# Masks and query decays of a retention layer: loaded tables, or products of small factors made on chip

## The chip, the cores and the metric

The kernel runs on one core of one Trainium2 chip. The metric is the device time of one execution in microseconds (us), the median of several runs. A core has five engines with their own instruction streams: TensorE (PE in the rows, its weight loads PEld), VectorE (DVE), ScalarE (ACT), GpSimd (POOL) and SyncE (SP), which here issues most of the DMAs. They meet at semaphores. TensorE writes its products into PSUM, eight banks of 512 numbers per partition; VectorE and ScalarE read them there.

## The reference, cut to what matters

The first layer is a retention (a linear attention with decay) over 4 batches, 8 heads, 576 positions and 64 features; two feed-forward layers follow (512 to 2048 and back, 2304 tokens).

```
scores = scale * q @ k.T                       # per batch and head
gamma  = 1.0 - 2.0 ** (-5.0 - arange(H))       # one decay per head
Dmat   = where(rel >= 0, gamma ** rel, 0.0)    # rel = row - column
x = (scores * Dmat) @ v                        # then heads side by side: 2304 x 512
h = x @ w_in;  g = max(0.01 * h, h);  x = g @ w_out
h = max(x @ w_in2, 0.0);              out = (h * h) @ w_out2
```

## The kernel before, in words

**Retention.** Each batch is cut into chunks, four of 128 positions and one of 64, so there are 20 chunks, and the loop goes over them in order (variable `i`). Within a chunk the scores of all heads are products of keys and queries (`scores`, L513), multiplied on VectorE by a mask that holds `gamma ** (t - s)` for s <= t and zero elsewhere (L515). Earlier chunks of the batch come in through a state per head, the sum of `k v` products (`sums`, L550, copied by ScalarE to `state`, L556). For that the keys are multiplied by `gk` (L528) and the queries by `gq` (L524), both on GpSimd. `gq` has one table for each chunk number 1 to 4 in a batch: `gamma ** (c * 128 + t)` times the scale. `output` adds the masked scores times values (L541) and the queries times state (L544) in one bank, and ScalarE copies it to `ysb` (L559), the input of the feed-forward layers.

**Tables.** Mask, `gq` and `gk` are computed on the host and loaded: the mask at L473, each `gq` at L470, `gk` at L477. The mask is 128 x 1024 numbers, a `gq` 128 x 512 (the last 128 x 256).

**Feed-forward.** The weights arrive as 64-bit floats and are taken apart by VectorE and ScalarE into high and low parts (`steps_in` L149 to L187, `steps_out` L191 to L216), in small steps that are spread among the chunks: `RATE` says how many steps stand behind a chunk, and `FIRST = 3` steps stand in front of the first. The first block of weights lands in `ysb`'s last third, which is still free (L128), and the later ones in `raw`. The feed-forward products (L318, L419) take three products per pair of operands; their operands are built by `operands` (L256 to L281), partly during the retention.

**Order.** The instructions of each engine run in the order of the program text; nothing reorders them. Each DMA in turn takes one of eight semaphores, and waits for the one that had it before. SP issues all DMAs here except the first three key loads, which ScalarE issues. Before the first scores TensorE makes products of a zero tile (`keep_warm`, L466), and again before the outputs of chunks 0 and 1; `WARM` holds the numbers.

**Banks.** Scores use two pairs of banks in turn (`wide`), sums have one bank for themselves. Output and warm-up products take the other three in turn, y1 to y3, and a tile that takes a bank waits until the reader of the last tile there is done:

```
def bank(name="yps", i=None):
    if i is None:
        i = turn[0] = turn[0] % 3 + 1 if att else (turn[0] + 1) % 4
    return psum.tile([P, 512], F32, tag=f"y{i}", name=name)
```

In the order of the calls warm-up products get y1, y2, output 0 y3, warm-up y1, output 1 y2, output 2 y3, output 3 y1. A product of 32-bit floats is carried out as two passes, so eight score products are 16 instructions in the trace.

Of the kernel before, what the change touches and what calls it, by code (L numbers as in the profile page):

```python
# [13 lines left out]
AF = mybir.ActivationFunctionType  # L14
# [3 lines left out]
B, H, S, D = 4, 8, 576, 64  # L18
NT, DM, DFF = B * S, H * D, 2048
P = 128  # L20
# [8 lines left out]
FULL = S // P  # L29
C = NP * P  # L30
# [5 lines left out]
DEEP = 4  # L36
# [4 lines left out]
ARRIVE = 3  # L41
FIRST = 3
AHEAD = 2
WARM = 10, 3, 1
BIGGEST = float(np.uint32(0x0FEFFFFF).view(np.float32))

A22, A11, A12, S1, S2, S3, S4 = range(7)


@with_exitstack  # L50
def retention_ffn_kernel(ctx: ExitStack, tc: tile.TileContext, full, rows, half, halfv, w1, w2, const, mask, gk, out):

# [9 lines left out]
    nc = tc.nc  # L64
    sub, mul, add, mx = ALU.subtract, ALU.mult, ALU.add, ALU.max
# [7 lines left out]
    ysb = [keep.tile([P, NK * 2 * HT], F32, name=f"ysb{i}") for i in range(NB)]  # L73
# [5 lines left out]
    def wide(i, name=None):  # L79

        return psum.tile([P, 2, 512], F32, tag="ab"[i], name=name or "ab"[i])
# [227 lines left out]
    def product(ps, ws, w, use, start):  # L309

        x = xs.pop(use)
        used[0] += 1
        for u in range(NU):
            hi, lo = ws[u]
            for k in range(2):
                s = slice(k * P, (k + 1) * P)
                for i, (a, b) in enumerate(((hi, 0), (hi, 1), (lo, 0))):
                    nc.tensor.matmul(  # L318
                        ps[:, u, :HT], a[:, w, s], x[:, b, k],
                        start=(start and k == 0 and i == 0), stop=(k == 1 and i == 2), skip_group_check=True,  # L320
                    )
        load_x()
# [122 lines left out]
    def tokens(i):  # L445
        b, c = chunks[i]
        return b * S + c * P, P if c < FULL else S - FULL * P

    class Retention:
# [15 lines left out]
                for _ in range(n):  # L465
                    nc.tensor.matmul(ps[:, :P], self.cold, self.cold, start=True, stop=True)  # L466

        def load_gq(self, c):
            src = const[c - 1].rearrange("p (a t) -> p a t", t=P)
            nc.sync.dma_start(self.gq[c - 1], src[:, :, : self.gq[c - 1].shape[2]])  # L470

        def load_mask(self):
            nc.sync.dma_start(self.mask.rearrange("p j a t -> p (j a t)"), mask)  # L473
            nc.vector.memset(self.state, 0.0)

        def load_gk(self):
            nc.sync.dma_start(self.gk.rearrange("p c h -> p (c h)"), gk)  # L477
# [90 lines left out]
    def run(n, limit):  # L568

        while n > 0 and done[0] < limit:  # L570
            if next(steps, None):
                break
            done[0] += 1
            n -= 1

    def build(n=1):

        ran = 0
        while builds and ran < n:
            try:  # L580
                if next(builds[0]):
                    break
                ran += 1
            except StopIteration:
                builds.pop(0)
        return ran

    GROUP = NU * (STEPS_IN + STEPS_OUT)
    with tc.manual_schedule():
        with tc.tile_pool(name="att", bufs=1) as pool:  # L590
            att.append(Retention(pool))
            ret = att[0]
            n = len(chunks)
            ret.load(0)
            ret.load_mask()
            ret.load_rows(0)
            ret.load_gk()
            weights.ahead()
            ret.load(1)
            ret.load_rows(1)  # L600
            ret.load_gq(1)
            ret.load(2)
            ret.load_rows(2)
            ret.load_gq(2)
            ret.load(3)
            ret.load_rows(3)
            ret.load_gq(3)
            ret.keep_warm(WARM[0])
            ret.scores(0)
            ret.decay(0)  # L610
            run(FIRST, GROUP)
            scored = 1
            for i in range(n):
                if i + DEEP < n:
                    ret.load(i + DEEP)
                    ret.load_rows(i + DEEP)
                    if i + DEEP <= FULL:
                        ret.load_gq(i + DEEP)
                if weights.loads < GRP and (weights.free or i == 1):
                    weights.free = False  # L620
                    weights.ahead()

                while scored < n and scored <= i + (AHEAD if i > 2 else min(i, 1)):
                    ret.scores(scored)
                    ret.decay(scored)
                    scored += 1
                ret.keep_warm(WARM[i + 1] if i + 1 < len(WARM) else 0)
                ret.output(i)
                a, t = tokens(i)
                if a < 2 * HT <= a + t:  # L630
                    builds.append(operands(0, 0))
                run(min(1, RATE[i]), GROUP - OWN)
                if BUILD[i] > 0:
                    build()
                run(RATE[i] - 1, GROUP - OWN)
                build(BUILD[i] - 1)
                if i >= n - 3 and i < n - 1:

                    early.append(wide(i - n + 3))
                    product(early[-1], [wt_in[0, 0], wt_in[0, 2]], (A11, A12)[i - n + 3], uses[i - n + 3], True)  # L640
                    if i == n - 3:
                        sums1 = stage.tile([P, NU, HT], F32, tag="t2", name="s")
                        nc.scalar.activation(sums1, early[0][:, :, :HT], AF.Copy)
                    else:
                        early.append(sums1)
# [12 lines left out]
        for layer in range(2):  # L658
            for g in range(NG):
                i = layer * NG + g  # L660


                start = i * GROUP + GROUP
# [46 lines left out]
def constants():  # L710

    gamma = (1.0 - 2.0 ** (-5.0 - np.arange(H, dtype=np.float32))).astype(np.float64)
    scale = 1 / np.sqrt(D)
    row, col = np.arange(P)[:, None], np.arange(C)[None, :]
    gq = [gamma[row // D + 2 * (col // P)] ** (c * P + col % P) * scale for c in range(1, FULL + 1)]
    since = col % P - row
    mask = [np.where(since >= 0, gamma[2 * (col // P) + j] ** np.maximum(since, 0) * scale, 0) for j in range(2)]
    gk = gamma ** -(np.arange(FULL)[:, None] * P + row[:, :, None]).astype(np.float64)
    return [a.astype(np.float32) for a in (np.stack(gq), np.concatenate(mask, axis=1), gk.reshape(P, -1))]


# [42 lines left out]
```

## Time and profile before

| | |
|---|---|
| median of 3 runs | 840.95 us (840.44 to 841.79) |
| the profiled execution: time, span | 840.44 us, 840.4 us |
| TensorE busy | 824.5 us (98%) |
| VectorE busy | 601.4 us (72%) |
| ScalarE busy | 340.2 us (40%) |
| GpSimd busy | 44.3 us (5%), all in the first 80 us |
| DMA over the span | 191.01 MB, 227 GB/s on average |

The time of an execution is its span, so nothing lies around it. The retention takes about the first 85 us; in it GpSimd works, and the DMA engines carry the inputs. The busy shares are averages over both stages, and TensorE's share is above 9 tenths in all but the first of 40 slices.

### The profile page before, as it was taken

Reading aid. Unit: us, or ns where it says so; the run is one execution under the profiler, and the core shown is the slowest. Engines: PE = TensorE matmul, PEld = TensorE weight load, DVE = VectorE, ACT = ScalarE, POOL = GpSimd, SP = SyncE. Lnnn points to the kernel's source line nnn. Section 1 sums busy time; section 2 is a strip of 40 time slices with the busy share of each in tenths; the row PEclk is TensorE's granted clock in tenths of the full one; section 3 lists DMA queues with packets and bytes.
Section 4 is the critical chain, followed back from the end, with each engine's and each line's share of the span. In section 5 each row is a group of like instructions: output and inputs, shape, how many; then the busy total and the mean of one; then the engine's idle time right before and its main releaser. Section 6 shows DMA issues by size and latency. Waiting matters only on the chain.

```text
span 840.4 us, 12382 instructions
## 1 busy us (share of the span) xinstructions
PE 824.5 (98%) x5084; PEld 776.9 (92%) x5084; DVE 601.4 (72%) x734; ACT 340.2 (40%) x447; POOL 44.3 (5%) x36
## 2 busy tenths in 40 slices
PE   7999999999999999999999999999999999999998
PEld 6888899999999999999999998998998998998996
DVE  4698789657666566658668879868777778754534
ACT  1454667544523433434425365543322333321211
POOL 3755000000000000000000000000000000000000
PEclk8999999999999999999999999999999999999999
DMA  9898463967646637746823554966855655735811
GB/s 349 330 322 292 170 258 114 420 250 260 247 180 250 248 135 292 259 140 233 307 101 122 191 226 163 385 246 233 296 178 203 263 182 231 263 140 199 288 51 75
DMA packets 45688, 191.01 MB, mean 227 GB/s; under 512 B 5696, under 2 KB 6720, under 8 KB 45632
## 3 DMA queue, kind: packets, MB, share of 16 engines
q1 hardware_dynamic: 45200, 189.44, 60.7%
q8 instruction: 40, 0.66, 0.3%
q10 hardware_dynamic: 432, 0.79, 0.3%
q14 instruction: 16, 0.13, 0.0%
HBM read 152.45 MB, written 37.75 MB: 226 GB/s over the span
## 4 chain that ended last, share of the span: by engine, by line
PE 84%; DVE 9%; ACT 3%; DMA 2%; issue 2%; SPq 0%; DVEq 0%; ACTq 0%
PE yps L419 44%; PE a L318 21%; PE b L318 15%; DMA raw<-in_w 1%; DVE r L515 1%; PE ops L544 1%; ACT sf L149 1%; PE ops L541 1%; DMA ysb<-in_w 1%; DVE x L260 1%; PE scps L513 1%; DVE sf L163 1%; DVE ilo L187 1%; PE sums L550 1%; DVE sf L205 1%
## 5 line engine op out<-in xcount | busy, mean ns | idle before, releaser
L318 PE MATMUL a<-x,ihi 128*128 128x384 f32 x768 | 196.1, 336 | 2.7 <-DVE t L384 2.4
L318 PE MATMUL b<-x,ihi 128*128 128x384 f32 x576 | 146.6, 335 | 0.8 <-DVE t L370 0.8
L318 PEld LDWEIGHTS a<-x,ihi 128*128 128x128 f32 x768 | 138.5, 188 | 5.8 <-DVE t L384 4.0
L419 PE MATMUL yps<-ghi,ohi 128*128 128x384 f32 x384 | 128.6, 335 | 0.6 <-ACT ysb L428 0.6
L318 PE MATMUL a<-x,ilo 128*128 128x384 f32 x384 | 128.5, 335 | 0.0
L419 PE MATMUL yps<-ghi,olo 128*128 128x384 f32 x384 | 128.3, 334 | 0.0
L419 PE MATMUL yps<-glo,ohi 128*128 128x384 f32 x384 | 128.3, 334 | 0.0
L356 DVE TENSOR_TENSOR glo<-t,ghi 128x768 fp32r<-128x768 f32 x96 | 91.7, 955 | 46.1 <-ACT ghi L351 45.6
L430 DVE TENSOR_TENSOR ysb<-yps,ysb 128x384 f32<-128x384 f32 (+1 forms) x126 | 76.0, 610 | 62.5 <-PE yps L419 62.1
L419 PE MATMUL yps<-ohi,glo 128*128 128x512 f32 x288 | 112.3, 390 | 0.0
L419 PE MATMUL yps<-olo,ghi 128*128 128x512 f32 x288 | 112.3, 390 | 0.0
L419 PE MATMUL yps<-ohi,ghi 128*128 128x512 f32 x288 | 112.1, 389 | 0.0
L351 ACT ACTIVATE ghi<-t 128x768 fp32r<-128x768 f32 x96 | 81.1, 845 | 68.5 <-DVE t L329 55.1
L318 PEld LDWEIGHTS b<-x,ihi 128*128 128x128 f32 x576 | 103.8, 188 | 1.7 <-DVE t L370 1.1
L344 ACT ACTIVATE s<-a 128x768 f32<-128x768 f32 x47 | 38.2, 814 | 156.2 <-PE a L318 156.1
L318 PE MATMUL b<-x,ilo 128*128 128x384 f32 x288 | 96.3, 334 | 0.0
L419 PEld LDWEIGHTS yps<-ghi,ohi 128*128 128x128 f32 x384 | 72.1, 188 | 1.6 <-ACT ysb L428 0.9
L318 PEld LDWEIGHTS a<-x,ilo 128*128 128x128 f32 x384 | 72.1, 188 | 0.0
L419 PEld LDWEIGHTS yps<-glo,ohi 128*128 128x128 f32 x384 | 72.1, 188 | 0.0
L419 PEld LDWEIGHTS yps<-ghi,olo 128*128 128x128 f32 x384 | 72.1, 188 | 0.0
L419 PEld LDWEIGHTS yps<-ohi,glo 128*128 128x128 f32 x288 | 54.0, 188 | 11.3
L419 PEld LDWEIGHTS yps<-olo,ghi 128*128 128x128 f32 x288 | 54.1, 188 | 11.0
(67 smaller groups left out, 997.3 us busy)
## 6 DMA issues: line engine op xcount, KB each, us to landing
x<-x SPq DMA_DIRECT2D x168, 768.0 KB, 5.9
raw<-in_w SPq DMA_DIRECT2D x62, 512.0 KB, 5.0
kv<-in_rows SPq DMA_DIRECT2D x16, 512.0 KB, 5.8
out<-ysb SPq DMA_DIRECT2D x18, 256.0 KB, 2.0
q<-in_full SPq DMA_DIRECT2D x16, 256.0 KB, 4.5
kt<-in_full SPq DMA_DIRECT2D x13, 256.0 KB, 4.7
ysb<-in_w SPq DMA_DIRECT2D x2, 512.0 KB, 6.8
kt<-in_full ACTq DMA_DIRECT2D x3, 256.0 KB, 5.6
```

What stands on the lines that cost most here:

```text
L149: nc.scalar.activation(f32(a), f32(raw[:, :, 1]), AF.Abs)
L163: nc.vector.scalar_tensor_tensor(a, high, 1 << 31, a, ALU.bitwise_and, ALU.bitwise_or)
L187: nc.vector.tensor_tensor(lo[:, a:z], sf[:, a + 1 : z + 1], f32(hi[:, a:z]), sub)
L205: nc.vector.scalar_tensor_tensor(rest, high, 23, low, ALU.logical_shift_left, ALU.bitwise_or)
L260: nc.vector.tensor_tensor(t[:, 1], src, f32(t[:, 0]), sub)
L318: nc.tensor.matmul(ps[:, u, :HT], a[:, w, s], x[:, b, k], start=(start and k == 0 and i == 0), stop=(k == 1 and i == 2), skip_group_check= ...
L344: nc.scalar.activation(t, ps[:, :, :HT], AF.Copy)
L351: nc.scalar.activation(h, t, AF.Copy)
L356: nc.vector.tensor_tensor(l, t, f32(gs[key][0]), sub)
L419: nc.tensor.matmul(acc, a, b, start=(j == u == i == 0), stop=(j == 1 and u == NU - 1 and i == 2))
L430: nc.vector.tensor_tensor(y, acc, y, add)
L513: nc.tensor.matmul(ps[:n, j, p, :n], k[s, c], q[s, c], start=True, stop=True)
```

## The change

The mask and the four `gq` tables are no longer loaded. Two small arrays are: `rank`, 8 partitions (one per head) by 1280 numbers, and `tri`, a 128 x 128 triangle of ones and zeros. Both lie in the second third of `ysb` until its rows are needed. Since `gamma ** (t - s)` is `gamma ** -s` times `gamma ** t`, a product over the 8 partitions, with zeros for the other heads, gives the whole table: `make_mask` makes two such products of 512 columns in a pair of banks, and VectorE multiplies them by the triangle into the mask. `make_gq(c)` makes one product of 512 columns in bank y3, and ScalarE copies it into `gq`. The mask and the first `gq` are made before chunk 0; `gq` 2, 3 and 4 are made after the outputs of chunks 0, 1 and 2. The first group of warm-up products has six instead of ten. Lines behind L474 move by 13 and later ones by more: scores are L526, outputs L554 and L557, sums L563, and ScalarE's copies L569 and L572.

```
-WARM = 10, 3, 1
+WARM = 6, 3, 1
...
-        def load_gq(self, c):
-            src = const[c - 1].rearrange("p (a t) -> p a t", t=P)
-            nc.sync.dma_start(self.gq[c - 1], src[:, :, : self.gq[c - 1].shape[2]])
-
-        def load_mask(self):
-            nc.sync.dma_start(self.mask.rearrange("p j a t -> p (j a t)"), mask)
+        def load_factors(self):
+            n = rank.shape[1]
+            self.rank, self.tri = ysb[1][:H, :n], ysb[1][:, n : n + P]
+            nc.sync.dma_start(self.rank, rank)
+            nc.scalar.dma_start(self.tri, tri)
             nc.vector.memset(self.state, 0.0)
+
+        def make_mask(self):
+            ps = wide(1, "mask")
+            for j in range(2):
+                nc.tensor.matmul(ps[:, j], self.rank[:, j * P : (j + 1) * P], self.rank[:, -C:], start=True, stop=True)
+            ps = ps.rearrange("p j (a t) -> p (j a) t", t=P)
+            tri = self.tri.unsqueeze(1).to_broadcast([P, H, P])
+            nc.vector.tensor_tensor(self.mask.rearrange("p j a t -> p (j a) t"), ps, tri, mul)
+
+        def make_gq(self, c):
+            ps = bank("decay", 3)
+            nc.tensor.matmul(ps, self.rank[:, (1 + c) * P : (2 + c) * P], self.rank[:, -C:], start=True, stop=True)
+            t = self.gq[c - 1]
+            nc.scalar.activation(t, ps.rearrange("p (a t) -> p a t", t=P)[:, :, : t.shape[2]], AF.Copy)
...
+            ret.load_factors()
             ret.load(0)
-            ret.load_mask()
             ret.load_rows(0)
...
             ret.load_rows(1)
-            ret.load_gq(1)
             ret.load(2)
             ret.load_rows(2)
-            ret.load_gq(2)
             ret.load(3)
             ret.load_rows(3)
-            ret.load_gq(3)
             ret.keep_warm(WARM[0])
+            ret.make_mask()
             ret.scores(0)
+            ret.make_gq(1)
             ret.decay(0)
...
-                    if i + DEEP <= FULL:
-                        ret.load_gq(i + DEEP)
...
                 ret.output(i)
+                if 2 + i <= FULL:
+                    ret.make_gq(2 + i)
...
+    rank = [(head % 2 == j) * gamma[:, None] ** -t for j in range(2)]
+    rank += [(head % 2 == t // D) * gamma[:, None] ** (c * P) for c in range(1, FULL + 1)]
+    rank += [(head // 2 == col // P) * gamma[:, None] ** (col % P) * scale]
+    tri = np.arange(P)[:, None] <= t
```

TensorE's first instructions, before (a name is that of the tile written, behind the arrow those read; scps are scores, cold the warm-up products, x10 is ten in a row):

```order
L466 MATMUL cold<-cold 128x128 x10
L513 MATMUL scps<-q,kt 128x128 x8
L466 MATMUL cold<-cold 128x128 x3
L541 MATMUL ops<-r,kv 64x128 x8
L550 MATMUL sums<-kv 64x64 x8
L513 MATMUL scps<-q,kt 128x128 x16
L466 MATMUL cold<-cold 128x128
L541 MATMUL ops<-r,kv 64x128 x8
```

And of the change, where decay is the product for a `gq` table:

```order
L466 MATMUL cold<-cold 128x128 x6
L478 MATMUL mask<-ysb_67 128x512 x2
L526 MATMUL scps<-q,kt 128x128 x8
L485 MATMUL decay<-ysb_67 128x512
L466 MATMUL cold<-cold 128x128 x3
L554 MATMUL ops<-r,kv 64x128 x8
L563 MATMUL sums<-kv 64x64 x8
L485 MATMUL decay<-ysb_67 128x512
L526 MATMUL scps<-q,kt 128x128 x16
L466 MATMUL cold<-cold 128x128
L554 MATMUL ops<-r,kv 64x128 x8
```

Two mask products stand in front of the first scores, a decay product behind them, and another between the sums of chunk 0 and the scores of chunks 1 and 2.

TensorE from the output of chunk 2 to the scores of chunks 4 and 5, before, with the semaphores that an instruction waits on (the number behind a name is that of one buffer):

```order
L541 MATMUL ops_260<-r_209,kv_109 64x128 [waits DMAHW5_49,DVE_49,Activation_49]
L541 MATMUL ops_260<-r_209,kv_109 64x128 x7
L544 MATMUL ops_260<-q_105,state_83 128x128 [waits Activation_49,Pool_49]
L544 MATMUL ops_260<-q_105,state_83 128x128 x3
L550 MATMUL sums_84<-kv_109 64x64 [waits Pool_49]
L550 MATMUL sums_84<-kv_109 64x64 x7
L513 MATMUL scps_293<-q_146,kt_147 64x64 [waits DMAHW4_49,DMAHW3_49,PE_49]
```

And of the change:

```order
L554 MATMUL ops_266<-r_212,kv_109 64x128 [waits DMAHW5_49,DVE_49,Activation_49]
L554 MATMUL ops_266<-r_212,kv_109 64x128 x7
L557 MATMUL ops_266<-q_105,state_83 128x128 [waits Pool_49]
L557 MATMUL ops_266<-q_105,state_83 128x128 x3
L563 MATMUL sums_84<-kv_109 64x64 [waits Pool_49]
L563 MATMUL sums_84<-kv_109 64x64 x7
L485 MATMUL decay_290<-ysb1_67 128x512 [waits PE_49,Activation_49]
L526 MATMUL scps_302<-q_147,kt_148 64x64 [waits DMAHW2_49,DMAHW1_49]
```

The fourth decay product stands in front of the scores of chunk 4 and waits for ScalarE (Activation), which reads bank y3.

ScalarE of the change, from the first `gq` copy on:

```order
L487 ACTIVATE gq_77<-decay 128x512
L149 ACTIVATE sf<-ysb_68 128x1024
L569 ACTIVATE state<-sums 64x4x64 x2
L572 ACTIVATE ysb_66<-ops 128x4x128
L487 ACTIVATE gq_78<-decay 128x512
L569 ACTIVATE state<-sums 64x4x64 x2
L572 ACTIVATE ysb_66<-ops 128x4x128
L487 ACTIVATE gq_79<-decay 128x512
L569 ACTIVATE state<-sums 64x4x64 x2
L572 ACTIVATE ysb_66<-ops 128x4x128
L487 ACTIVATE gq_80<-decay 128x256
```

Each of the later `gq` copies stands behind the state and output copies of a chunk; the first one stands in front of the conversion of the first weight block (L149).

## Rows read from the trace of the kernel before

**Rows 1.** Head of the page.
```profile
span 840.4 us, 12382 instructions
```

**Rows 2.** Busy time by stretch: stretch and length, each engine's busy time, clock, DMA.
```profile
38.90:71.30 32.40, 31.72 (x504) 28.12 (x504) 32.25 (x30) 14.62 (x29) 20.77 (x16) 1.00 0.83 287
85.00:840.00 755.00, 747.38 (x4036) 708.67 (x4034) 538.20 (x674) 303.95 (x379) 0.00 (x0) 1.00 0.58 216
```

**Rows 3.** Chain of waits, first 40 us: start, length, engine or DMA.
```profile
2.60 7.17 DMA ysb<-in_w
...
11.13 1.14 ACT sf L149
...
13.74 2.30 DVE sf L163
16.05 1.15 DVE r L515
...
17.24 1.98 PE ops L541 x16
...
22.27 1.58 PE scps L513 x16
23.85 1.02 PE ops L541 x16
...
26.57 1.70 PE scps L513 x32
28.28 1.02 PE ops L541 x16
...
31.01 1.09 PE scps L513 x16
```

**Rows 4.** Busy time by stretch, 10 to 23.2 us, engines PE, PEld, DVE, ACT, POOL.
```profile
10.00:12.80 2.80, 1.73 (x32) 1.43 (x32) 0.51 (x1) 2.77 (x4) 0.00 (x0) 1.00 1.03 408
12.80:16.40 3.60, 1.61 (x20) 1.30 (x18) 3.53 (x4) 0.72 (x2) 2.70 (x2) 1.00 1.04 410
16.40:23.20 6.80, 5.96 (x48) 5.29 (x50) 4.55 (x4) 0.77 (x3) 2.78 (x3) 0.50 1.08 377
```

**Rows 5.** DMA issues, first 20 us: count, KB each, us to landing.
```profile
gq<-in_const SPq DMA_DIRECT2D x3, 256.0 KB, 6.7
mask<-in_mask SPq DMA_DIRECT2D x1, 512.0 KB, 5.2
...
gq<-in_const SPq DMA_DIRECT2D x1, 128.0 KB, 6.0
```

**Rows 6.** Timeline of TensorE, first 7.3 us: start, length, instruction.
```profile
1.05 4.63 PE L466 MATMUL cold<-cold 128*128 128x128 f32 x20 [1.05 <-DVE cold L459]
5.62 1.42 PE L513 MATMUL scps<-q,kt 64*128 64x128 f32 x16
```

**Rows 7.** Groups by line and form, TensorE, 1 to 5.5 and 6.9 to 8 us.
```profile
L466 PE MATMUL cold<-cold 128*128 128x128 f32 x20 | 4.6, 429 | 1.1 <-DVE cold L459 1.1
...
L466 PE MATMUL cold<-cold 128*128 128x128 f32 x6 | 0.9, 292 | 0.0
```

**Rows 8.** DMA issues of the page: count, KB each, us to landing.
```profile
out<-ysb SPq DMA_DIRECT2D x18, 256.0 KB, 2.0
```

**Rows 9.** Line L487, first 30 us: query and key loads to landing.
```profile
DMA to landing us min/median/max: 3.6/5.8/6.9
```

**Rows 10.** Timeline of VectorE and ScalarE, 7 to 28 us.
```profile
7.08 1.23 DVE L515 TENSOR_TENSOR r<-scps,mask 128x1024 f32<-128x1024 f32 x1 [5.54 <-PE scps L513]
...
26.68 0.78 ACT L556 ACTIVATE state<-sums 64x256 f32<-64x256 f32 x2 [2.90 <-PE sums L550]
27.49 0.60 ACT L559 ACTIVATE ysb<-ops 128x512 f32<-128x512 f32 x1
```

**Rows 11.** Waits, first 40 us: total, times, longest.
```profile
PE scps L513 <- DMA q<-in_full: 2.6, 2, 1.5
...
PE ops L541 <- DVE r L515: 1.3, 1, 1.3
```

More of the change, by code (lines that the diff above doesn't have):

```diff
@@ L50, in retention_ffn_kernel @@
 @with_exitstack
-def retention_ffn_kernel(ctx: ExitStack, tc: tile.TileContext, full, rows, half, halfv, w1, w2, const, mask, gk, out):
+def retention_ffn_kernel(ctx: ExitStack, tc: tile.TileContext, full, rows, half, halfv, w1, w2, rank, tri, gk, out):
     nc = tc.nc
@@ L714, in constants @@
     row, col = np.arange(P)[:, None], np.arange(C)[None, :]
-    gq = [gamma[row // D + 2 * (col // P)] ** (c * P + col % P) * scale for c in range(1, FULL + 1)]
-    since = col % P - row
-    mask = [np.where(since >= 0, gamma[2 * (col // P) + j] ** np.maximum(since, 0) * scale, 0) for j in range(2)]
+    head, t = np.arange(H)[:, None], np.arange(P)[None, :]
+    rank = [(head % 2 == j) * gamma[:, None] ** -t for j in range(2)]
+    rank += [(head % 2 == t // D) * gamma[:, None] ** (c * P) for c in range(1, FULL + 1)]
+    rank += [(head // 2 == col // P) * gamma[:, None] ** (col % P) * scale]
+    tri = np.arange(P)[:, None] <= t
     gk = gamma ** -(np.arange(FULL)[:, None] * P + row[:, :, None]).astype(np.float64)
-    return [a.astype(np.float32) for a in (np.stack(gq), np.concatenate(mask, axis=1), gk.reshape(P, -1))]
+    return [a.astype(np.float32) for a in (np.concatenate(rank, axis=1), tri, gk.reshape(P, -1))]
 def kernel(q, k, v, moe_w_in, moe_w_out, moe2_w_in, moe2_w_out):
@@ L745, in weights @@
         return np.stack([a, w_out.reshape(NF, P, DM)], axis=1).view(np.int64)
-    const, mask, gk = constants()
+    rank, tri, gk = constants()
     arrays = {
@@ L750 @@
         "w1": weights(moe_w_in, moe_w_out), "w2": weights(moe2_w_in, moe2_w_out),
-        "const": const, "mask": mask, "gk": gk,
+        "rank": rank, "tri": tri, "gk": gk,
     }
```

## The prediction

> **What bounds the kernel now.** I read the page first: the span is 840.4 us [rows 1]. Then the busy time by stretch: from 85 us to 840 us TensorE is busy 747.4 of 755 us at the full clock [rows 2], and the change has no instruction there. So whatever it wins or loses it wins or loses before 85 us, as an earlier or later start of that stage, and the reader should expect microseconds, not per cents. Within the front part, VectorE is full from 38.9 to 71.3 us (32.25 of 32.40 us busy) [rows 2]; the change adds no VectorE work there, so this stretch is shifted as a block by whatever happens before it. That leaves the first 38 us.
>
> There I read the chain of waits [rows 3]. It runs over the landing of the first weight block (9.77 us), ScalarE's conversion (11.13), VectorE's three steps (to 16.05), the score multiply of chunk 1 that stands behind them on VectorE, and from 17.24 us over TensorE alone: output, state and sums of chunk 1 to 22.27, scores of chunk 3 to 23.85, output of chunk 2 to 26.57, scores of chunks 4 and 5 to 28.28, output of chunk 3. None of the replaced tables ends a wait on this chain; they sit in front of other transfers. The third thing is the clock: it is full in 10 to 16.4 us, though TensorE is busy there only 1.73 of 2.8 us and then 1.61 of 3.6 us, and it is 0.50, the 1.2 GHz level, from 16.4 to 23.2 us [rows 4]. The same output, state and sums that take 5.03 us for chunk 1 (17.24 to 22.27) take 2.72 us for chunk 2 (23.85 to 26.57) [rows 3]. The low clock costs the chain 2.3 us there and about 0.5 us in the scores behind (1.58 against 1.09), together 2.8 us.
>
> **The change part by part.** All times below are for the profiled execution, whose time is its span, 840.44 us; the median of the runs is 840.95 us, 0.5 us above, and I add that at the end.
>
> Transfers. Removed: the mask, 512 KB, and the decay tables, three of 256 KB and one of 128 KB [rows 5]; 1408 KB in all. Added: rank, 8 rows of 1280 numbers (40 KB), and tri (64 KB). The DMA engines are full and move about 410 GB/s [rows 4], so the first weight block, behind the mask in the queue, lands (512 - 104) KB / 410 GB/s = 1.0 us earlier. ScalarE's conversion goes from 11.13 to about 10.1 us and VectorE's steps end near 15.0 instead of 16.05 (part of it less if GpSimd, now later, leaves VectorE alone). Later loads come up to 3 us earlier, but after 17.24 us no DMA ends a wait on the chain, so that is worth nothing.
>
> Warm-up and mask products. Ten warm-up products take 4.63 us from 1.05 us [rows 6], 0.46 us each, two passes each, 429 ns a pass against 292 ns for the three products of 6.96 us [rows 7]: the page shows no level before 6 us, but the passes show the low one. The 16 score passes at 5.62 us take 1.42 us [rows 6] against about 1.16 in the record of later chunks (1.09 on the chain [rows 3]), so the clock rises near 6.1 us. Six products end near 3.7 us. A factor product has 512 columns, four times a warm-up product: 4 x 0.46 = 1.85 us at the low level, 0.93 at the full one. Two of them for the mask: from 3.75 to 6.1 us at the low level (64% of 3.70), the rest at the full one, end at 6.8. They need rank in time. Its landing has no row; the bounds are the 2.0 us from issue to landing of an output store with the queues nearly empty [rows 8] and the 3.6 us of the first 256 KB load [rows 9], so between 2.7 and 4.3 us for an issue at 0.74. I take 3 us, nearer the small one: before 3.7, no wait. The upper end costs 0.6 us.
> The Trainium skill (DMA: Bandwidth & Descriptors, Anatomy of one DMA, a fit for transfers that GpSimd issues) has about 2.0 us fixed plus the bytes over 436 GB/s: an estimate of 2.1 us for 40 KB, which would land rank at 2.8 us. No row here shows so small a load on an empty queue; by that rule the sum stays as it is, and the upper end of 0.6 us falls away.
>
> VectorE then multiplies the mask out of the product banks by the triangle: same shape and kind as the score multiply of 1.23 us [rows 10]; 6.95 to 8.2. Chunk 0's scores (1.09) are done at 7.9; its score multiply follows at 8.2 to 9.4, where before it began at 7.08 [rows 10]. The cover for that delay is the wait for the weight block.
>
> Decay products. The first (0.93) stands behind the scores: 8.8. ScalarE copies it (0.60, as the copy of an output [rows 10]), three warm-up products end at 9.6, output of chunk 0 runs 9.65 to 10.7, sums to 11.3. Now the banks matter. The copies of the decay product all use product bank 3, and output takes banks 1 to 3 in turn; chunk 0 and chunk 2 get bank 3. So the second decay product waits until ScalarE has copied the state (0.78) and the output (0.60) of chunk 0 [rows 10]: 11.3 + 0.1 + 0.78 + 0.60 + 0.15 = 12.95, end 13.9. Behind it on TensorE wait scores 1 and 2: 14.95 and 16.0. GpSimd's decay of query and key of chunk 1 follows scores 1, about 1 us later than now, with some tenths to spare. VectorE's score multiply 1 goes from 15.1 to 16.3; output 1 starts at **16.35 instead of 17.24: 0.9 us won**.
>
> The clock. TensorE now has the mask, decay products and earlier scores between 6 and 16 us: from 9.65 to 16.35 it idles only 1.7 and 0.1 us, against waits of 2.6 us (two, for queries) and 1.3 us (for the score multiply) in the same stretch before [rows 11]. I take it that the clock stays full: output, state and sums of chunk 1 take 2.72, to 19.07. **2.3 us won, and 0.5 in the scores.**
>
> The given back. Output 2 (bank 3) waits for the copy of decay product 3, which ScalarE makes after state (0.78) and output (0.60) of chunk 1: 0.1 + 0.78 + 0.60 + 0.60 + 0.15 + gaps = 2.3 us after the sums, 21.4; TensorE alone would need 0.93 + 1.09 = 2.0. It replaces the 1.58 between 22.27 and 23.85. Output 2 to sums 2: 2.72, 24.1. The fourth decay product waits for output 2's copy out of bank 3: 0.1 + 0.78 + 0.60 + 0.15 = 1.65, then 0.93: 26.7. Here nothing covers it, since TensorE had no wait here. Scores 4 and 5: 1.70, output 3 at **28.4 against 28.28**.
>
> So 0.9 + 2.3 + 0.5 = 3.7 us are won, and 3.8 are lost: 1.2 on the way to output 2 (2.3 for the 1.09 of the scores at the full clock) and 2.6 before the scores of chunk 4 (1.65 + 0.93). The sum is +0.1 us. From there everything is a shift of the same work. Forecast 840.44 + 0.1 = 840.5 for an execution like the profiled one, **841.0 at the median**. Bounds: with a column rate of the factor products 8% better (a product without its tail) and VectorE's long step at less than 2.30 us [rows 3], 0.6 us less; with rank late and GpSimd late, 0.9 more. Its own range is 840.3 to 842.0.
>
> **Rivals.**
> A. The clock falls as before, between 16 and 23 us. For it: the new idle places, 1.7 us before decay product 2 and 1.65 before product 4, are each longer than any single one of before (1.5 [rows 11]). Against: the work around them is denser than in the stretch that kept its clock at 1.73 of 2.8 us [rows 4]. Then chunk 1's part takes 5.03: 16.35 to 21.4; decay 3 at the low level 1.85, scores about 1.3: output 2 at 24.6, +2.72, +1.65 + 0.93 + 1.70 = 31.6 against 28.28: 3.3 us slower, 844.2. It decides from the point where the clock at output 1 is 0.50. This is the slower side.
> B. The clock rises late. If it is not up by 10 us, mask products end at 7.45, scores 0 at 9.1, decay 1 and the warm-up products at about 11.2, and with the bank wait output 1 starts near 17.9 instead of 16.35: 1.6 us, 842.5, more if it stays low longer. For it: six products instead of ten, and factor products that fill 8 of 128 rows. Against: TensorE has no longer pause than before in its first 6 us.
> The Trainium skill (TensorE: Matmul & The Clock Gate, What's actually happening) says that the low rate is the default and activity releases it; the 429 ns passes agree. Whether products with 8 rows count as such, no row here shows; if not, B holds.
> C. The bank waits are not on the path (ScalarE done early, or TensorE ahead elsewhere). Then output 3 starts at 16.35 + 2.72 + 0.93 + 1.09 + 2.72 + 0.93 + 1.70 = 26.4, 1.8 us earlier: 839.1, just faster by more than 0.2%. For it: ScalarE is little used here. Against: state and output copies can only start when the sums are done.
> D. The tables were hidden and so are their replacements: 840.95.
>
> **How the numbers follow.** 0.2% is 1.7 us, about what a measurement of this kernel can tell from no change. Forecast 0.49, A 0.17, B 0.12, C 0.17, D 0.05. Faster: C with most of its chance, and a tail of the forecast in which rank, mask and VectorE's steps all come early: 0.21. Slower: A, half of B, and a tail: 0.26. Same: 0.53. The time is the forecast's, 840.9 with D beside it. For 8 in 10 the range reaches to C below, 838.8, and to A above, 844.0.
>
> **What would show it.** Right: the clock at 1.00 from 6 to 30 us, mask products over near 6.8, output 1 near 16.4, a wait of TensorE of about 1.6 us in front of decay products 2 and 4 with ScalarE's output copy as releaser, output 3 near 28.3, and VectorE full after 39 as before. Wrong: 0.50 between 16 and 23 (A), low passes after 7 us (B), no wait before decay product 4 (C), or a chain that leaves the first 30 us for something that starts later, such as a load that lands out of its new order.

## The result: one per cent slower, and the profile after

| | before | after |
|---|---|---|
| median, 4 runs each | 841.04 us (840.44 to 841.79) | 849.24 us (848.39 to 851.24) |
| span of the profiled execution | 840.4 us | 846.6 us |

The ratio is 1.0100, with a 95% interval of 1.0088 to 1.0112: slower by 8.2 us at the median, and 5.2 us above the top of the predicted range. The profiled executions are 6.2 us apart. The other 2 us are a choice of executions: in all runs listed here the time is 1.8 us above the span (848.39 us against 846.6 us here), so by this estimate the profiled execution of before [rows 1] took about 842.2 us, 1.2 above its median, and that of after lies 0.85 below its own. The sentence ahead of the prediction that nothing lies around the span is wrong by these 1.8 us.

Head of the page of the changed kernel:

```profile
span 846.6 us, 12392 instructions
```

Busy time by stretch of the changed kernel, columns as in [rows 2] (stretch and length; PE, PEld, DVE, ACT, POOL busy with instructions; granted clock; DMA share and GB/s):

```profile
4.20:7.50 3.30, 3.30 (x21) 1.73 (x21) 1.37 (x2) 0.00 (x0) 0.00 (x0) 1.00 1.05 408
7.60:21.20 13.60, 12.10 (x80) 8.83 (x80) 5.77 (x6) 3.68 (x6) 3.60 (x4) 0.50 1.04 403
21.20:31.40 10.20, 8.64 (x104) 6.21 (x102) 7.47 (x7) 3.20 (x8) 5.65 (x4) 1.00 0.66 211
31.50:34.80 3.30, 3.30 (x38) 2.96 (x36) 1.12 (x2) 0.27 (x1) 1.72 (x2) 0.50 0.28 110
...
45.00:78.00 33.00, 32.15 (x508) 28.49 (x508) 32.64 (x30) 15.49 (x31) 21.43 (x15) 1.00 0.84 288
...
91.00:846.00 755.00, 747.33 (x4036) 708.68 (x4034) 538.01 (x674) 303.85 (x379) 0.00 (x0) 1.00 0.59 216
```

The last two lines answer to [rows 2]: VectorE is still full in its stretch, and the long stage takes the same 747.3 of 755 us. The whole difference is a later start, as expected. The first four lines answer to [rows 4], and there it is: 0.50, the 1.2 GHz level, for 13.7 us from 7.55 to 21.20 us, and again from 31.4 to 34.9 us, where before had one such stretch of 6.8 us. TensorE was not idle ahead of the first fall: it was busy in all 3.30 us from 4.2 to 7.5 us, and went on without a pause to 12.9 us.

Chain of waits of the changed kernel, first 36 us, answering to [rows 3] (start, length, engine, tile and line):

```profile
3.98 2.00 PE mask L478 x4
5.99 1.09 PE scps L526 x16
7.08 1.50 PE decay L485 x2
8.58 1.58 PE cold L466 x6
10.15 1.91 PE ops L554 x16
12.06 0.88 PE sums L563 x16
...
13.77 0.61 ACT ysb L572
...
14.42 2.07 PE decay L485 x2
16.48 3.71 PE scps L526 x32
20.20 0.72 PE cold L466 x2
20.92 1.18 PE ops L554 x16
...
23.80 1.05 PE decay L485 x2
24.85 1.09 PE scps L526 x16
25.95 1.02 PE ops L554 x16
...
30.23 1.12 PE decay L485 x2
31.35 2.96 PE scps L526 x32
34.31 1.30 PE ops L554 x16
```

The weight block and VectorE's three steps, which open this chain before, are gone from it. TensorE carries it from 1.05 us, with two visits to ScalarE (13 to 14.4 us, and the same in front of 30.23 us). Output 3 starts at 34.31 us instead of 28.28 [rows 3]: 6.0 of the 6.2 us between the spans. The decay product for chunk 2 takes 2.07 us, the next one 1.05; the 32 score passes at 16.48 take 3.71.

Timeline of VectorE and ScalarE in the changed kernel, answering to [rows 10] (start, length, engine, line, operation; in brackets idle time and what ended it):

```profile
6.03 1.23 DVE L481 TENSOR_TENSOR mask<-mask,ysb 128x1024 f32<-128x1024 f32 x1 [4.49 <-PE mask L478]
7.36 1.23 DVE L528 TENSOR_TENSOR r<-scps,mask 128x1024 f32<-128x1024 f32 x1
13.18 1.23 DVE L163 SCALAR_TENSOR_TENSOR sf<-ysb,sf 128x1024 uint32<-128x1024 uint32 x1
18.54 1.22 DVE L528 TENSOR_TENSOR r<-scps,mask 128x1024 f32<-128x1024 f32 x1 [4.13 <-PE scps L526]
...
2.60 1.28 ACT L487 ACT_TABLE_LOAD   x1 [2.60 <-issue]
10.56 1.14 ACT L149 ACTIVATE sf<-ysb 128x1024 f32<-128x1024 f32 x1 [1.35 <-DMA ysb<-in_w]
```

And the row of ScalarE's timeline in the kernel before that answers to the last two:

```profile
9.84 1.28 ACT L149 ACT_TABLE_LOAD   x1 [9.84 <-DMA ysb<-in_w]
```

The mask is there in time (output 0 does not wait for it), VectorE is done with the weight block at 14.4 us and then waits 4.13 us for TensorE's scores: the wait for the block became a wait for TensorE.

Waits of the changed kernel, first 60 us, answering to [rows 11] (engine and line, what it waited for, total us, times, longest):

```profile
PE decay L485 <- ACT ysb L572: 3.1, 2, 1.6
```

The two bank waits are real, and of the predicted length.

### The profile page after: what moved, and what is told of

Same layout as the page of the kernel before. It is cut to its first block, busy times and chain, and to the rows that moved or that the text cites. A ratio compares the mean times of both kernels' runs of the same rounds, so it can differ in the third digit from the quotient of the medians.

```text
span 846.6 us, 12392 instructions
## 1 busy us (share of the span) xinstructions
PE 832.6 (98%) x5088; PEld 779.8 (92%) x5088; DVE 601.3 (71%) x735; ACT 342.3 (40%) x451; POOL 45.9 (5%) x36
## 4 chain that ended last, share of the span: by engine, by line
PE 86%; DVE 8%; ACT 3%; issue 2%; DMA 1%; SPq 0%; DVEq 0%; ACTq 0%
PE yps L419 44%; PE a L318 21%; PE b L318 15%; PE scps L526 1%; DMA raw<-in_w 1%; PE ops L554 1%; PE ops L557 1%; DVE r L528 1%; ACT sf L149 1%; DVE x L260 1%; PE decay L485 1%; DVE ilo L187 1%; PE cold L466 1%; PE sums L563 1%; DVE sf L205 1%
```

## The experiments

After the result two reasons stood against each other. Theory 1, the clock: the mask and decay products fill 8 of 128 rows, and the claim is that TensorE's clock neither rises nor stays up behind such products. Its rival, the banks: the two waits for bank 3 make the chain longer, and the clock falls because TensorE pauses there. Differences below are medians against the median of before measured beside them (841.34, 840.58 and 840.51 us, 18 to 25 runs each); the change stands at +8.2 against its own four runs of before. Each record of the clock is that of one profiled execution.

**Rank over all 128 rows (e1).** The same products with zeros in the other 120 rows; `rank`'s load grows by this, and two memsets come with it.

```
-            self.rank, self.tri = ysb[1][:H, :n], ysb[1][:, n : n + P]
-            nc.sync.dma_start(self.rank, rank)
+            self.rank, self.tri = ysb[1][:, :n], ysb[1][:, n : n + P]
+            nc.sync.dma_start(self.rank[:32], rank)   # rows 8 to 31 are zeros
+            nc.vector.memset(self.rank[32:64], 0.0)
+            nc.gpsimd.memset(self.rank[64:], 0.0)
```

> The changed kernel with the factor products made over 128 rows instead of 8 (rank padded with zeros, the table values are the same); columns, number and order of products, bank waits and warm-up stay. Theory 1 (products that fill 8 rows do not hold the clock up): the clock that rose near 4 us stays at 1.00 through 7 to 30 us, decay product 1 takes about 0.9 instead of 1.5 us, output of chunk 3 starts near 28.4 instead of 34.3 us, and the time falls by 5 to 6 us, to within 1.5 us of the kernel before. Rival 2 (the idle waits for bank 3, or six instead of ten warm-up products, bring the clock down): the low stretch 7.5 to 21 us stays, the time stays within 1 us of the changed kernel, 7 to 8 us above the kernel before.

Measured: 844.13 us (842.78 to 848.13), ratio 1.0033 [1.0015, 1.0052]; +2.8 instead of +8.2. Busy time by stretch of this kernel:

```profile
4.00:14.20 10.20, 6.52 (x61) 4.12 (x61) 3.74 (x4) 2.95 (x5) 1.04 (x1) 1.00 1.01 373
14.25:17.60 3.35, 3.35 (x14) 1.85 (x16) 1.27 (x2) 0.60 (x1) 0.00 (x0) 0.50 1.05 402
```

And its timeline of TensorE:

```profile
6.93 1.13 PE L487 MATMUL decay<-ysb 128*128 128x512 f32 x2
...
14.18 2.06 PE L487 MATMUL decay<-ysb 128*128 128x512 f32 x2 [3.12 <-ACT ysb L574]
...
28.58 1.12 PE L487 MATMUL decay<-ysb 128*128 128x512 f32 x2 [1.56 <-ACT ysb L574]
29.64 1.77 PE L528 MATMUL scps<-q,kt 64*64 64x64 f32 x32
```

The clock now stays up past 7.55 us, and falls at 14.22 us, behind a pause of 3.12 us, for one short stretch. In front of the fourth decay product there is the same pause of 1.56 us as in the change, but the scores behind it take 1.77 us instead of 2.96: no fall. So the clock part of theory 1 held in this profile, and the size of what is won back was missed: 2.8 us remain. Four of the ten executions have a mean clock of 1.000 and still took 843.1 to 843.5 us, so about 2 us of the rest are no fall of the clock. Part of them the padding made itself: the weight block was issued at 3.96 us instead of 3.13, behind the landing of `tri` (`rank` beside it has 160 KB now instead of 40), ScalarE's conversion came at 11.72 us, and it stands in front of the copies that free bank 3.

**Other banks for the decay products (e2).** Rows as in the change; no pause before products 2 and 4.

```
-            ps = bank("decay", 3)
+            ps = bank("decay", (3, 2, 1, 2)[c - 1])
```

> The changed kernel with the decay products in banks 3, 2, 1, 2 instead of always 3, so that none waits for an output copy; rows stay 8. Theory 1: the clock still falls near 7.5 us and stays low to about 20 us, since nothing changes before; the waits of 1.5 us before decay products 2 and 4 go, 2 to 3 us of the 6 to 8 are won back, time 4 to 6 us above the kernel before. Rival 2 (the idle waits bring the clock down): at least the second low stretch at 31 us goes and the first is shorter than half, time within 2 us of the kernel before. A loss that was only the waits themselves: 3 us won back, clock rows unchanged.

Measured: 843.51 us (842.44 to 846.28), ratio 1.0024 [1.0009, 1.0039]; +2.2. Timeline of TensorE:

```profile
3.91 3.78 PE L478 MATMUL mask<-ysb 8*128 8x512 f32 x4
...
15.70 1.12 PE L485 MATMUL decay<-ysb 8*128 8x512 f32 x2
...
27.93 1.77 PE L526 MATMUL scps<-q,kt 64*64 64x64 f32 x32
29.63 1.09 PE L554 MATMUL ops<-r,kv 128*64 128x128 f32 x16
```

Nothing waits for a bank. The clock is low from the start (the four mask passes take 3.78 us, in the change 2.08) until 15.3 us and then stays up, behind the fourth decay product too. Theory 1 was missed here: it had 4 to 6 us left over, and 2.2 is close to what its rival named (within 2 us, no second fall). By the median other banks bring back as much as 128 rows. They do it in another way: both reach output 1 at the same time (19.34 us in e1, 19.28 in e2), but e1's chain comes over the late weight block and ScalarE's copies, and e2's over TensorE alone from 1.05 us, at the low clock until 15.3; from there e2 has no bank wait and is at output 3 by 29.63 us, e1 at 31.34. Of the second fall the profiles say: 8 rows without the pause did not bring it (e2), the pause without the 8 rows did not (e1), both together did (the change). For e2 all eight executions bear this out, with mean clocks of 0.999 and 1.000. Two of e1's ten have 0.995, lower than its profile's 0.998, and where the clock fell in them is not recorded.

**Both (e3).** The two edits above in one kernel.

> Both edits: factor products over 128 rows, and decay products in free banks. Theory 1: clock 1.00 from about 5 us on, no wait of TensorE for ScalarE's output copy, output of chunk 3 near 26.5 us against 28.3 before, time 1 to 2 us below the kernel before (839 to 840). Rival 2: no better than the banks edit alone.

Measured: 844.45 us (841.88 to 846.41), ratio 1.0033 [1.0013, 1.0053]; +3.1. The expectation was missed: the two repairs do not add up. Timeline of TensorE:

```profile
3.78 3.33 PE L480 MATMUL mask<-ysb 128*128 128x512 f32 x4
...
22.42 1.77 PE L487 MATMUL decay<-ysb 128*128 128x512 f32 x2
...
27.94 1.13 PE L487 MATMUL decay<-ysb 128*128 128x512 f32 x2
...
30.70 1.09 PE L556 MATMUL ops<-r,kv 128*64 128x128 f32 x16
```

The clock of this profile is that of before almost to the half microsecond (0.50 from 16.92 to 23.75 us, before 16.42 to 23.25), and output 3 starts at 30.70 us, in the same view of before at 28.21. What is left over are the decay products on TensorE's own path: the third takes 1.77 us, most of it at the low level, the fourth 1.13; 2.9 us together, more than the 2.5 that output 3 is late. Four of the five executions have a mean clock of 0.996 or 0.997; the fifth, with 0.999, took 841.88 us.

**Warm-up products over 8 rows in the kernel before (e4).** No table is touched.

```
-                nc.tensor.matmul(ps[:, :P], self.cold, self.cold, start=True, stop=True)
+                nc.tensor.matmul(ps[:, :P], self.cold[:H], self.cold[:H], start=True, stop=True)
```

> The kernel before (tables loaded) with its fourteen warm-up products over 8 rows of the zero tile instead of 128; nothing else changes, the output is the same. Theory 1: the passes stay at the low level (429 ns) through the ten products and the first scores, and the clock is still low when output of chunk 0 runs at 8.5 us, where before it was full from about 6 us; time 0 to 4 us above the kernel before. Rival 2 (columns and gaps count, not rows): the clock rises near 6 us as before and the time is the same.

One run: 840.52 us (-0.8). Timeline of TensorE:

```profile
5.61 2.08 PE L513 MATMUL scps<-q,kt 64*128 64x128 f32 x16
...
9.19 1.98 PE L541 MATMUL ops<-r,kv 128*64 128x128 f32 x16
...
14.33 1.16 PE L513 MATMUL scps<-q,kt 64*128 64x128 f32 x16 [0.30 <-DMA q<-in_full]
...
24.48 1.09 PE L541 MATMUL ops<-r,kv 128*64 128x128 f32 x16
```

The same twenty passes, back to back from 1.05 to 5.6 us, and six more at 7.62 us, over 8 rows instead of 128: the clock comes up at 14.05 instead of 6.18 us. With the twenty passes over 128 rows it also came up at 6.36 us in e6 and at 5.09 in e10 (both below); over 8 rows there is this one execution. The operands are zeros in both kernels, so here the difference lies in the rows a product takes in, not in the numbers. And the second half: the time, as far as one execution tells, is no worse. The clock stays up from 14.05 us on, and output 3 starts at 24.48, 3.7 us earlier than in the profile of before; the span is 1.7 us shorter, since TensorE then waits for a key load until 28.79 us. The low clock of the first 14 us is not on the path here: the chain of this execution runs over loads up to that point. The fall from 16.4 to 23.3 us was on the path of before.

**Mask half alone (e5), decay half alone (e6).** e5 makes the mask from factors with six warm-up products, and loads the `gq` tables; e6 loads the mask, has ten warm-up products, and makes the `gq` tables as the change does.

```
e5:  -            ret.make_gq(1)
     +            ret.load_gq(1)         # 2 to 4 likewise, where before has them
e6:  -            ret.make_mask()        # and the mask's load back; first load(0), then the factors
     -WARM = 6, 3, 1
     +WARM = 10, 3, 1
```

> Half of the change: the mask made from factors (8 rows, six warm-up products), the four decay tables loaded as before. Theory 1 (8-row products let the clock fall, and the decay products with their bank waits spread the damage over 12 to 35 us): without decay products TensorE has no 8-row product after 6 us and no wait for an output copy, so output of chunk 3 starts within 1.5 us of 28.3 and the time is within 1.5 us of the kernel before. Rival 3 (the mask's own path, factors, products and multiply, is what comes late): 3 us or more above the kernel before.

> The other half: the mask loaded as before with ten warm-up products, the decay tables made from factors (8 rows, always bank 3). Theory 1: two waits of 1.5 us for the output copies and four products of 1.05 to 2.1 us on TensorE, a lower clock behind them: 4 to 8 us above the kernel before, most of the change's loss. Rival 3: less than 2 us above.

Measured: e5 839.15 us (837.16 to 844.37), ratio 0.9984 [0.9965, 1.0003], -1.4; e6 846.64 us (845.86 to 848.58), ratio 1.0075 [1.0058, 1.0092], +6.1. Timeline of TensorE in e5:

```profile
3.91 3.78 PE L478 MATMUL mask<-ysb 8*128 8x512 f32 x4
...
13.59 2.06 PE L524 MATMUL scps<-q,kt 64*128 64x128 f32 x32
```

And in e6:

```profile
13.54 2.07 PE L485 MATMUL decay<-ysb 8*128 8x512 f32 x2 [3.02 <-ACT ysb L572]
15.53 3.79 PE L526 MATMUL scps<-q,kt 64*128 64x128 f32 x32
...
29.20 1.12 PE L485 MATMUL decay<-ysb 8*128 8x512 f32 x2 [1.56 <-ACT ysb L572]
30.25 3.12 PE L526 MATMUL scps<-q,kt 64*64 64x64 f32 x32
33.30 1.25 PE L554 MATMUL ops<-r,kv 128*64 128x128 f32 x16
```

The decay half alone makes three quarters of the loss, with both falls (0.50 from 13.19 to 20.01 and from 30.25 to 33.67 us) at its bank waits. The first of these came in the wait of 3.02 us itself, before the 8-row product, as in e1 behind 3.12 us; so it needs no 8 rows. The mask half shows no loss; that it gains is not shown, since its interval holds 1. In its profile the clock is low until 13.1 us and up from there, and the chain of that execution runs over the weight block and VectorE until output 1, so the low clock is not on it. The halves do not add up: -1.4 and +6.1 make 4.7, not 8.2. That fits the chains: in the change TensorE carries the chain from 1.05 us, and the low clock behind the mask products is on it.

**Six warm-up products in the kernel before (e7).** `WARM = 6, 3, 1`.

> The kernel before with six instead of ten warm-up products in the first group, nothing else. Theory 1: the chain of the first 17 us runs over the weight block, and the clock of before is lost at 16 us anyway, so the time is within 1 us of the kernel before. Rival 2 (the warm-up's number is what counts): 3 us or more above.

Measured: 841.49 us (839.85 to 845.04), ratio 1.0011 [0.9995, 1.0027]: no effect that can be told.

**Decay products where TensorE waits anyway (e8).** From e3: products 1 and 2 behind scores 0, products 3 and 4 behind sums 0, banks 3, 1, 3, 1, and only the first warm-up group; so the pauses go and the products leave the stretch behind output 1.

```
-WARM = 6, 3, 1
+WARM = (6,)
             ret.make_gq(1)
+            ret.make_gq(2)
...
-                if 2 + i <= FULL:
-                    ret.make_gq(2 + i)
+                if i == 0:
+                    ret.make_gq(3)
+                    ret.make_gq(4)
```

> All tables from factors over 128 rows, the decay products moved to where TensorE waits anyway: products 1 and 2 behind the first scores, 3 and 4 behind the sums of chunk 0, in banks 3, 1, 3, 1, and the warm-up groups of three and one left out. If what the edits of rows and banks leave (2 to 3 us above the kernel before) is the two decay products that stand on TensorE's path between outputs 1 and 3, it goes: output of chunk 3 starts at or before 27 us, time 0 to 3 us below the kernel before. If it is something else, such as the later weight block, the time stays 2 to 3 us above.

Measured: 839.96 us (837.46 to 841.87), ratio 0.9993 [0.9979, 1.0007]; level with before, 3.7 us below e3 in difference to its own before. Timeline of TensorE:

```profile
18.28 1.09 PE L556 MATMUL ops<-r,kv 128*64 128x128 f32 x16 [2.42 <-issue]
...
26.53 1.09 PE L556 MATMUL ops<-r,kv 128*64 128x128 f32 x16
```

In the profile the clock is up from 6.2 us on. This fits the reading of e3, that the rest was the place of the products, but does not separate it from the clock: this profile has no fall, e3's has one, and the mean clock is 0.998 or more in nine of ten executions here and in one of five there. The later warm-up groups went in the same edit, too. Output 1 comes 2.42 us behind the last scores; the row names no releaser, but VectorE's score multiplies start at 16.96 us, behind steps on the weight block whose conversion on ScalarE comes at 12.24 us.

**Warm-up products before output 1 (e10, e11).** In the kernel before (`WARM = 10, 3, 6`) and in e5 (`WARM = 6, 3, 6`): six full products in the wait ahead of output 1, against before's own fall at 16.4 us.

> The kernel before with six instead of one warm-up product in front of output 1, where TensorE waits for the score multiply (1.3 us); nothing else. If the clock's fall at 16 us is what costs the 2.8 us that the prediction reckoned, and the work in that wait keeps the clock up, the record has no 0.50 between 10 and 30 us and the time is 1.5 to 3 us below the kernel before. If the fall has another cause, the record and the time stay as before, within 0.7 us.

> The mask from factors, the decay tables loaded, and six warm-up products in front of output 1: the version that the runs so far point to. Mask alone came out 1.4 us below the kernel before, with a few executions 2 to 4 us above in which the clock fell. Expected: 2 to 3.5 us below the kernel before, with less spread. If the products in front of output 1 come to stand on the path (scores late at the low clock), the gain over the mask alone is nothing.

Measured: e10 840.41 us (838.65 to 842.93), ratio 1.0000 [0.9983, 1.0018]; e11 839.54 us (838.31 to 842.73), ratio 0.9992 [0.9976, 1.0008]. Timeline of TensorE in e10:

```profile
25.34 1.09 PE L541 MATMUL ops<-r,kv 128*64 128x128 f32 x16
```

In the profile of e10 the clock is up from 5.09 us through the whole retention, and output 3 starts 2.9 us earlier than before; but the median is that of before. The profiled execution, 839.44 us, is one of ten, and before has such executions too: its 19 runs beside these go from 837.82 to 843.55 us. A mean clock of 0.998 or less, which says that it fell somewhere, stands beside 14 of those 19 and beside 5 of the ten of e10. So the fall of before [rows 4] comes in many of its executions and not in all, and six more products do not take it away; whether they make it rarer is too few runs to tell. The gain forecast for e10 was missed at the median, that for e11 too: it is no better than e5.

**The change once more (e12).** Beside e10 and e11.

> The changed kernel once more, beside the same runs of the kernel before as the two others. Theory 1, as measured: 7 to 9 us above the kernel before, with the clock falling right behind the mask and decay products and again behind decay product 4. If the first measurement was of one unlucky place of the clock's changes in the program, 2 to 4 us above.

Measured: 848.46 us (847.97 to 849.77), ratio 1.0103 [1.0076, 1.0131]. The loss is there again in another set of runs. The record of the clock is another one: up from 4.69, 0.50 from 8.10 to 11.52, from 14.93 to 18.34 and from 28.58 to 35.41 us. Where the clock falls moves by some microseconds; that it falls behind 8-row products, with TensorE busy without a pause (7.55 and 8.10 us), and again at the fourth decay product is in both.

## Why the prediction was wrong, step by step

Starts and lengths in us, predicted and measured (chain of waits of after):

| step | predicted | measured |
|---|---|---|
| mask products end | 6.8 | 5.99 |
| scores 0 end | 7.9 | 7.08 |
| output 0 starts | 9.65 | 10.15 |
| output 0 and sums | 1.65 | 2.79 |
| wait for bank 3 | 1.65 | 1.48 |
| decay 2 | 0.95 | 2.06 |
| scores 1 and 2 | 2.1 | 3.72 |
| output 1 starts | 16.35 | 20.92 |
| output 1 to sums 1 | 2.72 | 2.88 |
| on to output 2 | 2.3 | 2.15 |
| output 2 to sums 2 | 2.72 | 2.75 |
| wait for bank 3 | 1.65 | 1.53 |
| decay 4 | 0.93 | 1.12 |
| scores 4 and 5 | 1.70 | 2.96 |
| output 3 starts | 28.4 | 34.31 |

**The step that failed** is "I take it that the clock stays full". It is written in front of output 1, but the sum uses full-clock lengths from 6.1 us on, and there it broke. Output 1 is 4.6 us late: 1.1 in output 0 and sums, 1.1 in decay 2, 1.6 in the scores, 0.4 in the warm-up product at 20.20 us, 0.5 ahead of output 0, less 0.2 for the shorter wait; all the long ones lie between 7.55 and 21.20 us at 0.50. Another 1.3 us are lost in scores 4 and 5, at 0.50 again. With the few tenths of the other rows that is the 5.9 us between 28.4 and 34.3. I argued from idle time alone: TensorE would pause less than before, so the clock would stay. It was busy without a gap ahead of the first fall. What differs is the rows of its products. Eight profiles begin on TensorE with the same six warm-up products, mask products and scores, and differ up to there only in the rows of the mask products:

| clock at the mask products | over 8 rows | over 128 rows |
|---|---|---|
| up by 4.7 us | falls at 7.55 (change), 8.10 (e12) | stays to 14.22 (e1) |
| not up yet | up at 15.31 (e2), 13.10 (e5), 11.66 (e11) | up at 6.68 (e3), 6.21 (e8) |

With e4 that is the evidence that the rows decide in this first stretch: behind products over 8 rows the clock was not raised or held, behind the same products over 128 rows it was. By the Trainium skill (TensorE: Matmul & The Clock Gate, What's actually happening) the low rate is the default and activity releases it; the traces agree, and 8-row products did not release it here.

**Rivals A and B** each had a part, and neither came as written. B named the 8 rows, the cause in the first stretch, but its late rise did not happen in this profile: the clock was up at 4.14 us and fell again (in e2, e5 and e11 the rise was late). A had a fall, but from 16 us on, and most of its price lay in chunk 1 from output to sums, which took 2.88 us, not 5.03. The fall at 7.55 us under full work, and the second one at decay 4, neither had. B's "more if it stays low longer" had no price, and the range ended at A alone; yet A and B together, 844.2 and 1.6, would still be 3.4 us short of 849.24.

**The bank waits** came where and as long as forecast (1.50 and 1.56 us by the timeline), and the steps from output 1 to the fourth decay product came out within 0.2 us each. What I did not see is that a pause is not only its own length: at the 1.56 us in front of decay 4, with its 8 rows, the clock went too in the change, e6 and e12, and in e1's profile, with 128 rows, it did not. e6 shows what the decay products and their waits cost without the mask products: +6.1.

**"2.3 won and 0.5 in the scores"**: at their place, yes; output 1 to sums 1 took 2.88 us instead of 5.03, since the clock was up again by 21.2 us. The low stretch had moved ahead of it and grown.

**The weight block** was sized at 1.0 us earlier. ScalarE's conversion came 0.57 earlier (10.56), as the sum of two things I had not seen. The block landed near 10.5 us, 0.7 later than 9.77: its issue waited for `tri`, whose semaphore it takes over. And ScalarE's table load of 1.28 us, which before began when the block had landed (9.84), now stands at 2.60 in front of the first `gq` copy, where ScalarE had nothing to do. VectorE's L163 took 1.23 us instead of 2.30 [rows 3], with GpSimd idle beside it until 18.64 us; I had put that under bounds. All of it was won in vain: VectorE waited 4.13 us for scores.

**Rank and mask**: no wait for rank, mask multiply 1.23 us as the row said. The mask products ended 0.8 us earlier than forecast, because the clock was up at 4.14 us and not at the 6.1 taken; in e2 the same four passes took 3.78 us at the low level. One reading of the prediction is loose: 429 ns is the length of a warm-up pass that overlaps the next one, and twenty passes take 4.63 us, so two of them are not 0.86 us; the sum used the right 0.46 us per product.

**What is shown and what stays open.** Shown: 8-row products left the clock low in the first stretch (the table of eight profiles, and e4), the decay half alone makes most of the loss (e6), the low clock and the waits and decay products on TensorE's path make up the 6 us of the profile (the table of steps; e1, e2 and e3 take parts of them away). Not shown: how many rows are enough (nothing between 8 and 128 was run; the scores take in 64, but never stood alone); why the two repairs of e3 together leave 3.1 us, with a fall at 16.92 us that e2 does not have; and what decides from execution to execution whether before keeps its clock. The Trainium skill (same page, same section) says that the number of slow products at the start differs from run to run of one kernel; the change agrees, with the first full stretch beginning at 4.14 us in one profile and 4.69 in the other, and e2, which has the same instructions on TensorE up to there, has none before 15.3. So single records of the clock bear less weight than the medians. The mean clock of a run helps only one way, below 1: a low stretch ahead of the first record shows as 1.00, as in e2. Of the four executions of the change those with 0.990 took 848.4 and 848.6 us, those with 0.996 and 0.998 took 849.9 and 851.2; a low start that is not recorded, as in e2, would explain this order, but no profile shows it.

No version clearly beats the kernel before. Nearest is the mask from factors with the decay tables loaded (e5): 0.9984 [0.9965, 1.0003].

## What to carry to other kernels

Before small products replace a loaded table, look at how many rows they take in and at what they wait for, not only at how long they last: of the 8.2 us that they cost this kernel, zero rows up to 128 gave back 5.4, and banks whose last reader was done gave back 6.0, though not both together. Whether a low clock costs time depends on the chain: in e5 the same mask products left it low for 13 us without a loss that can be told. Place such products where TensorE waits for something else anyway (e8, level with before). And a rival that says "more if it lasts longer" needs a price for that before the range is closed.

## What the runs showed of the hardware that was not expected

- Twenty back-to-back passes over 8 rows, and six more behind the scores, left the clock at 1.2 GHz until 14.05 us (e4, one execution); over 128 rows, all zeros too, it rose at 6.18 us (before), 6.36 (e6) and 5.09 (e10).
- With the clock up, TensorE busy without a pause on products over 8 rows and scores between them, it fell at 7.55 us (change) and 8.10 us (e12); over 128 rows it stayed up to 14.22 us, where it fell behind a pause of 3.12 us (e1).
- A pause of 1.56 us in front of a product of 128 rows left the clock up (e1, one profile); the same pause in front of an 8-row product went with a fall (change, e6, e12).
- A low clock for the first 13 to 14 us was not on the chain in e4 and e5, and no loss shows; in e2 the chain runs over TensorE from 1.05 us, through the low clock until 15.3 us. Without the fall at 16 to 23 us output 3 came 2.9 us earlier (e10's profile).
- ScalarE's first activation brought a table load of 1.28 us. In the kernel before it stood at 9.84 us, behind the landing that this activation waits for; in the change at 2.60 us, 6 us ahead of its data. Why it waited in one and not in the other is open.
